# Chunked attention and a Mish feed-forward layer: accumulators copied out one at a time, an earlier load of q and k, and attention steps moved by half a slot

## The chip, the cores and the metric

The kernel runs on one core of one Trainium2 chip. The metric is the device time of one execution in microseconds, the median of several runs. The engines are called by their names in the profile: PE is TensorE, PEld its weight loads, DVE is VectorE, ACT is ScalarE, SP is SyncE, which issues nearly all DMAs here (SPq is its queue of DMA issues), and POOL is GpSimd, which only makes the identity matrix.

## The reference

q, k and v are 8 x 8 heads x 576 positions x 64, in float32. Attention works in chunks of 64 positions that see only themselves; its output, laid out as 4608 tokens of 512, goes through a feed-forward layer of width 2048:

```python
scores = scale * np.matmul(q_c, k_c.transpose(0, 1, 2, 4, 3))
scores = scores - np.max(scores, axis=-1, keepdims=True)
attn = np.exp(scores)
attn = attn / (np.sum(attn, axis=-1, keepdims=True) + 1e-09)
out = np.matmul(attn, v_c)
...
h = x @ w_in
sp = np.where(h > 20.0, h, np.log1p(np.exp(np.minimum(h, 20.0))))
g = h * np.tanh(sp)
return (g @ w_out).astype(np.float32)
```

## The kernel before

**Precision.** The large matmuls take operands in a rounded float32 (fp32r). Each operand is split into a high part (a cast) and a low part (a subtraction), and a product takes three matmuls: low x high, high x low, high x high. So each tile of activations costs one cast and one subtraction of 128x512 before PE can use it. The names end accordingly: `gh` and `gl` are the two parts of the activated hidden tile g, `wo_h` and `wo_l` those of w_out.

**Tiles and blocks.** A pair is 256 tokens; there are 18 pairs. The hidden layer has 16 tiles of 128 (f = 0 to 15). The work goes by blocks of tokens: a first block of pairs 0 and 1 (512 tokens), then blocks 1 to 4 with four pairs (1024 tokens) each.

*The first block* is `prologue` (attention of pairs 0 and 1, first weights) and 16 calls of `slot` (L583 to L622). Each slot does one f: a matmul chain `up` (L419) makes h, ACT applies Mish, `g_split` (L434) makes gh and gl, and `down` queues 12 matmuls (4 token tiles t = 0 to 3 times three parts) that add g @ w_out into the accumulators. Beside that the slot takes in the weights: they come as 64-bit words, ACT scales, DVE puts bits together (`w_bits`, L116), ACT casts the high part, DVE subtracts for the low part (`w_lo`, L140). The attention of pairs 2 to 5, which block 1 needs, is spread over the slots as well. Its steps stand in two plans, `on_pe` and `beside_pe` (L555 to L577), whose keys count half slots: scores, max and subtraction (L254, L266), exponential (L275), sum and reciprocal (L280), normalisation `a_norm` (L287), transposes `a_transpose` (L296), their copy out `a_copy` (ps, L307), the product with v `a_values` (av, L228) and its copy out `a_raw` (raw, L317).

*Blocks 1 to 4* replace the plain product x @ w_in by a scheme with seven products of half size (`PRODUCTS`, L626) on sums of parts of x (`x_step`: splits x_B, x_T at L373 and L374, sums raw at L379) and of parts of the weights. `s_build(u)` (L183) makes the weight sums for unit u: four DVE operations (L196), an ACT cast (L198), a DVE subtraction (L199) and a store, all in one buffer `bld`. `load_op` (L640) loads one operand of the products, from the plain parts (w_A) or the sums (w_S). Per block there are 8 calls of `unit` (L671), each for two f and both halves of the block's tokens. A unit's seven products go to three PSUM tiles in turn, x, y and v, from a pool of two; ACT copies x out (L682, L704, L716), DVE adds y and v to what was copied (`add`, L666), and ACT applies Mish (L432). Between the products a unit works off the queue `fill` by `filled(n)` (L465): n of the matmuls that earlier `down` calls queued. They belong to the first half of the block's tokens; the second half's activations stay in the buffer `zb` until `phase_two` (L746), which takes them f by f. In blocks 1 to 3 the units also carry the attention of the next block's pairs (one pair for two units), and `phase_two` its x_steps.

**Accumulators.** `acc[0]` to `acc[3]` are the four token tiles of the half in work. They lie in two PSUM tiles of two banks each: o0 holds t = 0 and 1, o2 holds t = 2 and 3, as these lines of `down_mm` show:

```python
if f == 0 and n == 0 and t % 2 == 0:
    o = ps_o.tile([P, 2, DM], F32, name=f"o_{key}_{t}", tag=f"o{t}")
    acc[t], acc[t + 1] = o[:, 0], o[:, 1]
```

`store` (L469) copies all four out to buffers `ob`, even t on ACT (L475), odd t on DVE (L473), and sends each with two DMAs on SP's queue (L479). The buffers are from the pool `c` with three buffers. It is called in unit 0 of each block, after the fifth product and ahead of `a_norm` (for the second half of the block before), in `phase_two` at f = 1 (for the first half), and at the end.

**Order.** The kernel runs under a manual schedule: each engine, and SP's queue, works in the order in which the code issues, and the framework adds the semaphore waits. q, k, v, p and ps of most pairs share the pool `at` with three buffers.

## Time and profile before

| | |
|---|---|
| median of 3 runs | 900.29 us (899.21 to 901.59) |
| the profiled execution, its own time | 900.59 us |
| its span, first to last instruction | 898.8 us |
| mean granted PE clock | 0.969 |
| ACT busy | 387.9 us (43%) |
| DMA, mean over the span | 153 GB/s, 137.25 MB |

The stages, by stretches of the span, with PE's busy time, the time that it stands still, DVE's and ACT's busy time (us) and PE's granted clock:

| stretch | what runs | PE | idle | DVE | ACT | clock |
|---|---|---|---|---|---|---|
| 0 to 54 | prologue, slots 0 to 2 | 35.44 | 18.56 | 40.23 | 35.56 | 0.88 |
| 54 to 160 | the other slots | 82.56 | 23.44 | 87.87 | 73.96 | 0.90 |
| 160 to 186 | start and unit 0 of block 1 | 18.13 | 7.87 | 10.45 | 8.42 | 0.83 |
| 186 to 306 | units of block 1 | 118.83 | 1.17 | 60.36 | 52.31 | 0.99 |
| 306 to 318 | start of its second half | 10.43 | 1.57 | 7.16 | 4.58 | 1.00 |
| 351 to 371 | start and unit 0 of block 2 | 16.47 | 3.53 | 9.83 | 8.73 | 1.00 |
| 371 to 489 | units of block 2 | 117.97 | 0.03 | 46.13 | 47.88 | 1.00 |
| 489 to 500 | start of its second half | 9.41 | 1.59 | 6.20 | 4.87 | 1.00 |
| 535 to 555 | start and unit 0 of block 3 | 16.45 | 3.55 | 10.56 | 8.45 | 0.96 |
| 680 to 690 | start of its second half | 8.37 | 1.63 | 6.61 | 3.39 | 1.00 |
| 842 to 852 | the same in block 4 | 8.55 | 1.45 | 3.04 | 2.94 | 1.00 |
| 852 to 899 | the end | 39.89 | 7.11 | 10.85 | 9.28 | 0.96 |

A row of the timeline gives start and length in us, engine, line, operation, output<-inputs, sizes and the number of instructions taken together; in square brackets stands how long the engine had stood idle just before, and what released it. A row of the list of waits gives the waiting engine and line, what it waited for, the total in us, how many times, and the longest. A row of a group gives line, engine, operation, count, busy time and mean of one in ns, then the idle time just before and its releasers.

### The profile page before, as it was taken

To read this page: it belongs to the slowest core of one execution; us is meant where nothing else is said; L and a number is where in the kernel's file an instruction comes from. 1 tells how busy PE (TensorE), PEld (TensorE's weight loads), DVE (VectorE), ACT (ScalarE), POOL (GpSimd) and SP (SyncE) were. 2 spreads that over 40 slices of the span, in tenths; PEclk is the share of its full clock that TensorE was granted. 3 is DMA by queue.
4 is the path that set the end of the run, shared out by engine and by line. 5 is a ranking of instruction groups with operands and counts; after the bars stand their busy time and mean duration, and the time that the engine had idled before them with its cause. 6 is when DMAs were issued, how large, how long until landed. Compare 5 with 4: busy or idle time off the path is not lost.

```text
span 898.8 us, 14182 instructions
## 1 busy us (share of the span) xinstructions
PE 827.2 (92%) x5724; PEld 675.1 (75%) x5724; DVE 438.7 (49%) x678; ACT 387.9 (43%) x584; POOL 0.7 (0%) x6
## 2 busy tenths in 40 slices
PE   4979974689999999899999998999999999999996
PEld 4757763567888788688888786888887888888785
DVE  6878997357435364442443644335336532323322
ACT  4778964335444343443443434344334332222221
POOL 0000000000000000000000000000000000000000
PEclk9889988799999999999999998999999999999999
DMA  7879944599855421656553305555532045444202
GB/s 269 321 266 324 314 171 170 170 303 306 273 159 137 107 66 48 182 140 174 161 140 96 94 19 146 176 153 141 177 107 70 1 115 153 128 120 118 47 1 47
DMA packets 68577, 137.25 MB, mean 153 GB/s; under 512 B 7072, under 2 KB 13216, under 8 KB 67488
## 3 DMA queue, kind: packets, MB, share of 16 engines
q1 hardware_dynamic: 68224, 135.82, 49.8%
q8 instruction: 46, 0.75, 0.3%
q10 hardware_dynamic: 288, 0.52, 0.2%
q14 instruction: 19, 0.16, 0.1%
HBM read 108.00 MB, written 28.31 MB: 152 GB/s over the span
## 4 chain that ended last, share of the span: by engine, by line
PE 77%; DVE 9%; ACT 6%; DMA 5%; issue 3%; SPq 0%; DVEq 0%; ACTq 0%
PE x L654 18%; PE v L654 9%; PE y L654 5%; PE o_(4, 0)_0_6431 L452 2%; PE o_(3, 0)_0_4943 L452 2%; PE o_(1, 1)_2_2947 L452 2%; PE o_(3, 1)_2_6043 L452 2%; PE o_(2, 1)_2_4495 L452 2%; PE o_(4, 1)_2_7188 L452 2%; PE o_(3, 0)_2_4960 L452 2%; PE o_(2, 0)_2_3412 L452 2%; PE o_(4, 1)_0_7181 L452 2%; PE o_(2, 0)_0_3395 L452 2%; PE o_(4, 0)_2_6448 L452 2%; PE av L228 2%
## 5 line engine op out<-in xcount | busy, mean ns | idle before, releaser
L666 DVE TENSOR_TENSOR zb<-v,zb 128x512 f32<-128x512 f32 x64 | 44.2, 690 | 121.2 <-ACT zb L716 64.1
L654 PE MATMUL x<-x_T,w_S 128*128 128x512 f32 x384 | 99.2, 394 | 0.6 <-ACT zb L704 0.6
L654 PEld LDWEIGHTS x<-x_T,w_S 128*128 128x128 f32 x384 | 71.1, 188 | 16.1 <-ACT zb L704 1.1
L666 DVE TENSOR_TENSOR z<-y,z 128x512 f32<-128x512 f32 x32 | 22.1, 692 | 101.3 <-PE y L654 99.3
L432 ACT ACTIVATE zb<-zb 128x512 f32<-128x512 f32 x64 | 40.5, 632 | 70.8 <-DVE zb L666 70.7
L439 DVE CAST gh<-z 128x512 fp32r<-128x512 f32 x72 | 30.6, 425 | 67.0 <-PE o_(4, 0)_2_6448 L452 19.0
L441 DVE TENSOR_TENSOR gl<-z,gh 128x512 fp32r<-128x512 f32 x80 | 55.3, 692 | 13.7 <-ACT gh L437 11.2
L716 ACT COPY zb<-x 128x512 f32<-128x512 f32 x32 | 18.8, 586 | 95.6 <-PE x L654 95.6
L432 ACT ACTIVATE z<-z 128x512 f32<-128x512 f32 x32 | 20.2, 631 | 91.9 <-DVE z L666 91.9
L296 PE MATMUL pt<-ident,p 128*128 128x128 f32 x144 | 23.7, 315 | 32.7 <-DVE p L287 18.9
L654 PE MATMUL x<-x_B,w_A 128*128 128x512 f32 x192 | 52.6, 410 | 0.9 <-ACT x_B L373 0.7
L654 PE MATMUL y<-x_B,w_A 128*128 128x512 f32 x192 | 51.6, 405 | 0.6 <-DVE zb L666 0.6
L419 PE MATMUL h<-x_first,wi 128*128 128x512 f32 (+1 forms) x204 | 50.5, 401 | 0.7 <-ACT x_first L336 0.7
L654 PE MATMUL v<-x_B,w_S 128*128 128x512 f32 x192 | 48.9, 390 | 0.2 <-DVE zb L666 0.2
L654 PE MATMUL x<-x_T,w_A 128*128 128x512 f32 x192 | 48.9, 390 | 0.1
L654 PE MATMUL v<-x_T,w_S 128*128 128x512 f32 x192 | 48.7, 389 | 0.0
L296 PEld LDWEIGHTS pt<-ident,p 128*128 128x128 f32 x144 | 19.4, 162 | 37.7 <-issue 22.9
L419 PEld LDWEIGHTS h<-x_first,wi 128*128 128x128 f32 x204 | 39.0, 206 | 8.4 <-ACT x_first L336 0.9
L654 PEld LDWEIGHTS y<-x_B,w_A 128*128 128x128 f32 x192 | 35.8, 193 | 9.6 <-DVE zb L666 1.8
L654 PEld LDWEIGHTS x<-x_B,w_A 128*128 128x128 f32 x192 | 36.4, 196 | 8.7 <-ACT x_B L373 1.1
L228 PE MATMUL s<-k,q 64*64 64x64 f32 x1088 | 21.7, 232 | 22.7 <-DMA k<-in_k 22.6
L654 PEld LDWEIGHTS v<-x_B,w_S 128*128 128x128 f32 x192 | 36.0, 188 | 8.0 <-DVE zb L666 0.6
(197 smaller groups left out, 1770.3 us busy)
## 6 DMA issues: line engine op xcount, KB each, us to landing
w_S<-sa SPq DMA_DIRECT2D x128, 256.0 KB, 3.2
w_A<-ra SPq DMA_DIRECT2D x96, 256.0 KB, 2.7
wst<-in_w_in SPq DMA_DIRECT2D x16, 512.0 KB, 5.5
wst<-in_w_out SPq DMA_DIRECT2D x16, 512.0 KB, 5.2
q<-in_q SPq DMA_DIRECT2D x16, 512.0 KB, 4.0
k<-in_k SPq DMA_DIRECT2D x16, 512.0 KB, 4.6
v<-in_v SPq DMA_DIRECT2D x16, 512.0 KB, 4.7
sa<-bld SPq DMA_DIRECT2D x8, 1024.0 KB, 5.0
```

The source lines that it names most:

```text
L228: nc.tensor.matmul(o[h * CHUNK : (h + 1) * CHUNK, c, t - ts.start, g], lhsT=l[rows, t, 2 * g + h], rhs=r[rows, t, 2 * g + h], start=True, ...
L296: nc.tensor.transpose(out=d["pt", ts.start][:, t - ts.start, g], in_=d["p"][:, t, g].rearrange("p c k -> p (c k)"), identity=ident,)
L419: nc.tensor.matmul(h[:, cols], lhsT=wi[i][:, w_, kt], rhs=x[:, x_, kt, cols], start=(n == 0), stop=(n == 3 * NK - 1),)
L432: nc.scalar.activation(out=out_, in_=in_, func=AF.Mish)
L439: nc.vector.tensor_copy(out=d["gh"], in_=z)
L441: nc.vector.tensor_tensor(out=d["gl"], in0=z, in1=d["gh"].bitcast(F32), op=ALU.subtract)
L452: nc.tensor.matmul(acc[t], lhsT=g[:, t * P : (t + 1) * P], rhs=w_[:, f], start=(f == 0 and n == 0), stop=(f == NF - 1 and n == 2),)
L654: nc.tensor.matmul(o, lhsT=t[:, w_, kt], rhs=x[x_][:, kt], start=(start and i == 0), stop=(i == 5), skip_group_check=not start,)
L666: nc.vector.tensor_tensor(out=z, in0=o, in1=z, op=ALU.add)
L716: nc.scalar.copy(out=b2, in_=x)
```

## The change

1. **Copies out.** `store` takes one t. In unit 0 of a block the matmuls still in `fill` (24 in block 1, 12 in the others) are spread over the first five products (3, 3, 2, 2 and 2 twelfths), and `stores`, called at four places, copies out each accumulator whose last matmul has been issued. In block 1 that is t = 0 behind `a_exp` and the other three behind `a_norm`; in blocks 2 to 4 t = 0 behind the first copy, t = 1 behind `a_exp`, the other two behind `a_norm`. In `phase_two` at f = 0 the last 12 matmuls of the first half are issued three at a time, each three followed by the copy of their accumulator. At the end the last 24 matmuls are sorted by token tile; six are issued, then that accumulator is copied in two halves, one on ACT and one on DVE, ACT's half with its own DMAs on ACT's queue.
2. **g_split earlier.** In `phase_two` each f's `g_split` stands ahead of the 12 matmuls of the f before it; in every unit the second `g_split` stands ahead of the unit's last `add` and Mish.
3. **q and k of the first pair of block 2** (pair 6) are loaded at the end of slot 14, ahead of both `s_build` calls and of four `load_op`; before, behind `s_build(1)` at the end of slot 15. The half slot's attention steps stand ahead of `s_build` too.
4. **Half a slot.** Transposes, ps, av and raw of pair 2 and all steps of pairs 3 to 5 (the load of their q and k too) come one key, that is half a slot, later, and so does the first part of the steps on x's second half.
5. **Which engine casts gh in the slots.** Before ACT in even slots; now in the slots of `BY_SCALAR`.

```diff
-    def store(key, pairs):
-        for t in range(TOK // P):
...
+    def by_token():
+        fill.sort(key=lambda x: x[3])
+
+    stored = {}
+
+    def stores(key, pairs):
+        done = TOK // P - -(-len(fill) // 3)
+        for t in range(stored.setdefault(key, 0), done):
+            store(key, pairs, t)
+            stored[key] += 1
+
+    def store(key, pairs, t, cuts=1):
+        o = c_p.tile([P, DM], F32, name=f"ob_{key}_{t}", tag="c")
+        half, c = divmod(t, 2)
+        for n in range(cuts):
+            cols = slice(n * DM // cuts, (n + 1) * DM // cuts)
+            on_vector = (t + n) % 2
+            if on_vector:
+                nc.vector.tensor_copy(out=o[:, cols], in_=acc[t][:, cols])
             else:
-                nc.scalar.copy(out=o, in_=acc[t])
...
+                nc.scalar.copy(out=o[:, cols], in_=acc[t][:, cols])
+            queue = nc.scalar if cuts > 1 and not on_vector else nc.sync
...
-    for i, h0 in enumerate((1, 8, 15, 22)):
+    for i, (h0, h1) in enumerate(((1, 7), (9, 14), (16, 21), (23, 28))):
...
-    beside_pe.setdefault(29, []).extend((lambda n: x_step(1, 1, n), n) for n in range(5))
+    beside_pe.setdefault(30, []).extend((lambda n: x_step(1, 1, n), n) for n in range(5))
...
+    BY_SCALAR = (1, 3, 5, 7, 8, 10, 12, 14)
...
-        g_split(it[s], it[s]["z"], f"0_{s}", s % 2 == 0)
+        g_split(it[s], it[s]["z"], f"0_{s}", s in BY_SCALAR)
...
+        run(beside_pe, 2 * s + 1)
         if s == NF - 2:
+            load_qk(first_pair(2))
             s_build(0)
             for i in range(LOOK - 2):
                 load_op()
-        run(beside_pe, 2 * s + 1)
         if s == NF - 1:
             s_build(1)
-            load_qk(first_pair(2))
...
+            parts = [left * n // 12 for n in (3, 3, 2, 2, 2)]
...
         if begins:
             a_scores(j)
             load_v(j)
+        if u == 0:
+            stores(key, pairs)
...
         if begins:
             a_exp(j)
+        if u == 0:
+            stores(key, pairs)
...
-        if u == 0:
-            if m == 1:
-                store("0", (0, 1))
-            else:
-                p = first_pair(m - 1)
-                store(f"{m - 1}b", (p + 1, p + 3))
         if begins:
             a_norm(j)
+        if u == 0:
+            stores(key, pairs)
         product(m, u, 5, x, False)
         a2["z"] = z_tile(f"z_{m}_{2 * u + 1}")
         mish(a2["z"], x)
+        if u == 0:
+            stores(key, pairs)
...
         filled()
+        g_split(a2, a2["z"], f"{m}_{2 * u + 1}")
         add(y, b1)
         mish(b1, b1)
-        g_split(a2, a2["z"], f"{m}_{2 * u + 1}")
...
-            filled(12)
-            if f == 1:
-                store(f"{m}a", (p, p + 2))
             d = {}
+            if f == 0:
+                filled(12)
             g_split(d, z_of(f), f"{m}b_{f}", True)
+            if f == 0:
+                for t in range(TOK // P):
+                    filled(3)
+                    store(f"{m}a", (p, p + 2), t)
+            elif after or f < NF - 1:
+                filled(12)
...
-        filled()
+        by_token()
         p = first_pair(QUADS)
-        store("last", (p + 1, p + 3))
+        for t in range(TOK // P):
+            filled(6)
+            store("last", (p + 1, p + 3), t, 2)
```

The order on DVE at the end of the slots, slots 14 and 15, before. `woc` and `wo_l` (L116, L140) are the last tiles of w_out, p at L287 is pair 5's, raw, x_T and x_B belong to the second half of block 1's x, L196 and L199 are the first weight sums:

```order
L287 TENSOR_TENSOR p_1361<-p_1361,r_0_1416 128x2x8x64
L116 SCALAR_TENSOR_TENSOR woc_1446<-woc_1446,wst 128x512
L116 SCALAR_TENSOR_TENSOR woc_1446<-wst,woc_1446 128x512
L140 TENSOR_TENSOR wo_l<-woc_1409,wo_h 128x512
L374 TENSOR_TENSOR x_T_1_1490<-raw_715,x_T_0_1488 128x4x2x64
L441 TENSOR_TENSOR gl_14_1541<-z_1474,gh_14_1539 128x512
L140 TENSOR_TENSOR wo_l<-woc_1446,wo_h 128x512
L196 TENSOR_TENSOR bld<-bld 128x256 x4
L199 TENSOR_TENSOR bld<-bld 128x4x256
L374 TENSOR_TENSOR x_T_1_1578<-raw_715,x_T_0_1576 128x4x2x64
L374 TENSOR_TENSOR x_B_1_1166<-raw_1266,x_B_0_1164 128x4x2x64
```

and the same stretch in the changed kernel:

```order
L116 SCALAR_TENSOR_TENSOR woc_1442<-woc_1442,wst 128x512
L116 SCALAR_TENSOR_TENSOR woc_1442<-wst,woc_1442 128x512
L140 TENSOR_TENSOR wo_l<-woc_1408,wo_h 128x512
L287 TENSOR_TENSOR p_1390<-p_1390,r_0_1448 128x2x8x64
L374 TENSOR_TENSOR x_T_1_1479<-raw_741,x_T_0_1477 128x4x2x64
L441 TENSOR_TENSOR gl_14_1506<-z_1464,gh_14_1504 128x512
L140 TENSOR_TENSOR wo_l<-woc_1442,wo_h 128x512
L374 TENSOR_TENSOR x_T_1_1562<-raw_741,x_T_0_1560 128x4x2x64
L196 TENSOR_TENSOR bld<-bld 128x256 x4
L199 TENSOR_TENSOR bld<-bld 128x4x256
L439 CAST gh_15_1584<-z_1556 128x512
L441 TENSOR_TENSOR gl_15_1586<-z_1556,gh_15_1584 128x512
```

p of pair 5 (L287) now stands behind the two bit operations and one subtraction more. The second x_T, which stood behind the sums, stands ahead of them, and behind the sums come gh and gl of slot 15, whose cast was on ACT before.

The order on PE at the start of block 1's second half, with the semaphores that are waited for. o_(1, 0)_0 holds accumulators 0 and 1, o_(1, 0)_2 accumulators 2 and 3; the rows are the last matmuls of the first half (f = 15), three for each accumulator. Before:

```order
L452 MATMUL o_(1, 0)_0_1808<-wo_h_98,gl_1_15_2877 128x512 [waits DVE_49]
L452 MATMUL o_(1, 0)_0_1808<-wo_l_99,gh_1_15_2875 128x512
L452 MATMUL o_(1, 0)_0_1808<-wo_h_98,gh_1_15_2875 128x512
L452 MATMUL o_(1, 0)_0_1808<-wo_h_98,gl_1_15_2877 128x512
L452 MATMUL o_(1, 0)_0_1808<-wo_l_99,gh_1_15_2875 128x512
L452 MATMUL o_(1, 0)_0_1808<-wo_h_98,gh_1_15_2875 128x512
L452 MATMUL o_(1, 0)_2_1825<-wo_h_98,gl_1_15_2877 128x512
```

and changed:

```order
L452 MATMUL o_(1, 0)_0_1808<-wo_h_98,gl_1_15_2875 128x512 [waits DVE_49]
L452 MATMUL o_(1, 0)_0_1808<-wo_l_99,gh_1_15_2873 128x512
L452 MATMUL o_(1, 0)_0_1808<-wo_h_98,gh_1_15_2873 128x512
L452 MATMUL o_(1, 0)_0_1808<-wo_h_98,gl_1_15_2875 128x512 [waits Activation_49]
L452 MATMUL o_(1, 0)_0_1808<-wo_l_99,gh_1_15_2873 128x512
L452 MATMUL o_(1, 0)_0_1808<-wo_h_98,gh_1_15_2873 128x512
L452 MATMUL o_(1, 0)_2_1825<-wo_h_98,gl_1_15_2875 128x512
```

Between the third and the fourth row, from accumulator 0 to accumulator 1, PE now waits for a semaphore of ACT. The same stands between accumulators 2 and 3.

The order on DVE at the end of unit 1 of block 1. The first `zb` belongs to the sum that frees v's bank, gh_1_3 and gl_1_3 to the unit's second tile. Before:

```order
L196 TENSOR_TENSOR bld_1484<-bld_1484 128x256 x4
L199 TENSOR_TENSOR bld_1484<-bld_1484 128x4x256
L666 TENSOR_TENSOR zb_1_0_1614<-v_1_1_1890,zb_1_0_1614 128x512
L439 CAST gh_1_3_1954<-z_1_3_1931 128x512
L441 TENSOR_TENSOR gl_1_3_1956<-z_1_3_1931,gh_1_3_1954 128x512
L666 TENSOR_TENSOR z_1_4_1958<-y_1_2_2007,z_1_4_1958 128x512
```

and changed:

```order
L196 TENSOR_TENSOR bld_1474<-bld_1474 128x256 x4
L199 TENSOR_TENSOR bld_1474<-bld_1474 128x4x256
L439 CAST gh_1_3_1952<-z_1_3_1931 128x512
L441 TENSOR_TENSOR gl_1_3_1954<-z_1_3_1931,gh_1_3_1952 128x512
L682 TENSOR_TENSOR zb_1_0_1614<-v_1_1_1890,zb_1_0_1614 128x512
L682 TENSOR_TENSOR z_1_4_1958<-y_1_2_2007,z_1_4_1958 128x512
```

The cast and the subtraction for gh and gl now stand ahead of the add to zb.

More of the change, by code (lines that the diff above doesn't have):

```diff
@@ L467, in filled @@
             down_mm(*fill.pop(0))
-    def store(key, pairs):
-        for t in range(TOK // P):
-            o = c_p.tile([P, DM], F32, name=f"ob_{key}_{t}", tag="c")
-            if t % 2:
-                nc.vector.tensor_copy(out=o, in_=acc[t])
-            else:
-                nc.scalar.copy(out=o, in_=acc[t])
-            half, c = divmod(t, 2)
+    def by_token():
[14 more added lines that the diff above has]
+                nc.vector.tensor_copy(out=o[:, cols], in_=acc[t][:, cols])
+            else:
+                nc.scalar.copy(out=o[:, cols], in_=acc[t][:, cols])
+            queue = nc.scalar if cuts > 1 and not on_vector else nc.sync
             for i in range(2):
                 r = (pairs[half] * 2 + i) * P + c * CHUNK
-                nc.sync.dma_start(
-                    out=out[r : r + CHUNK, :], in_=o[i * CHUNK : (i + 1) * CHUNK]
+                queue.dma_start(
+                    out=out[r : r + CHUNK, cols], in_=o[i * CHUNK : (i + 1) * CHUNK, cols]
                 )
@@ L555 @@
     on_pe, beside_pe = {}, {}
-    for i, h0 in enumerate((1, 8, 15, 22)):
+    for i, (h0, h1) in enumerate(((1, 7), (9, 14), (16, 21), (23, 28))):
         j = first_pair(1) + i
-        for n, step in ((0, a_scores), (5, a_transpose), (6, a_values)):
+        for n, step in ((0, a_scores), (h1 - h0, a_transpose), (h1 - h0 + 1, a_values)):
             on_pe.setdefault(h0 + n, []).append((step, j))
@@ L565 @@
             (4, (a_norm,)),
-            (5, (a_copy,)),
-            (6, (a_raw,)),
+            (h1 - h0, (a_copy,)),
+            (h1 - h0 + 1, (a_raw,)),
         ):
@@ L677, in unit @@
         a1, a2 = {"z": z_tile(f"z_{m}_{2 * u}")}, {}
+        left = len(fill)
+        if u == 0:
+            parts = [left * n // 12 for n in (3, 3, 2, 2, 2)]
+            if m == 1:
+                key, pairs = "0", (0, 1)
+            else:
+                p = first_pair(m - 1)
+                key, pairs = f"{m - 1}b", (p + 1, p + 3)
         x = ps_h.tile([P, TOK], F32, name=f"x_{m}_{u}", tag="h")
         product(m, u, 0, x, True)
-        filled(3)
+        filled(parts[0] if u == 0 else 3)
         nc.scalar.copy(out=a1["z"], in_=x)
@@ L685, in unit @@
             load_v(j)
+        if u == 0:
+            stores(key, pairs)
         y = ps_h.tile([P, TOK], F32, name=f"y_{m}_{u}", tag="h")
         product(m, u, 1, y, True)
-        filled(5)
+        filled(parts[1] if u == 0 else 5)
         add(y, a1["z"])
@@ L702, in unit @@
         product(m, u, 2, x, False)
-        filled(4)
+        filled(parts[2] if u == 0 else 4)
         nc.scalar.copy(out=b1, in_=x)
@@ L706, in unit @@
             a_exp(j)
+        if u == 0:
+            stores(key, pairs)
         y = ps_h.tile([P, TOK], F32, name=f"v_{m}_{u}", tag="h")
         product(m, u, 3, y, True)
-        filled(4)
+        filled(parts[3] if u == 0 else 4)
         g_split(a1, a1["z"], f"{m}_{2 * u}")
@@ L729, in unit @@
         mish(a2["z"], x)
+        if u == 0:
+            stores(key, pairs)
         if m == 1 and (u, 1) in BUILDS:
```

## The prediction

> **What bounds the kernel now.** I read the busy times first, then the list of who waited for whom, then the instructions in order of time where PE (TensorE) stands still. In the first fence come the page's busy line, then wait rows: engine and line, what it waited for, total us, times, longest.
>
> ```profile
> PE 827.2 (92%) x5724; PEld 675.1 (75%) x5724; DVE 438.7 (49%) x678; ACT 387.9 (43%) x584; POOL 0.7 (0%) x6
> ...
> PE s L228 <- DMA k<-in_k: 22.6, 2, 17.9
> PE pt L296 <- DVE p L287: 18.9, 5, 5.9
> PE o_(4, 1)_2_7188 L452 <- DVE ob_4a L473: 1.4, 1, 1.4
> PE o_(1, 1)_2_2947 L452 <- DVE ob_1a L473: 1.0, 1, 1.0
> PE o_(1, 1)_0_2940 L452 <- DVE ob_1a L473: 0.5, 1, 0.5
> DVE gl L441 <- ACT gh L437: 11.2, 5, 4.3
> ```
>
> PE is busy 827.2 of 898.8 us, and its number of matmuls does not change, so only the 71.6 us of standing still can be won (and what a slowed clock costs behind them). The largest wait is one of 17.9 us for k, then the transposes that wait for the normalised p (DVE, VectorE). The copies of the accumulators cost PE little directly, about 1.5 us at each of four places, but DVE waits inside them. In the first block PE waits for DVE, and DVE in turn stands 11.2 us for casts on ACT (ScalarE). Times are summed against the profiled execution, 900.6 us (span 898.8 and 1.8 around it); the median of the runs, 900.29, is 0.3 lower.
>
> **Part 1: k, and what is late behind it.** The instructions around the wait (start, us, engine, line; in brackets idle time before and its releaser):
>
> ```profile
> 131.94 1.22 DVE L287 TENSOR_TENSOR p<-p,r 128x1024 f32<-128x1024 f32 x1
> 133.31 1.94 PE L296 MATMUL pt<-ident,p 128*128 128x128 f32 x8 [5.93 <-DVE p L287]
> 134.90 3.98 PE L419 MATMUL h<-x_first,wi 128*128 128x512 f32 x12
> 138.80 1.16 PE L228 MATMUL av<-ps,v 64*64 64x64 f32 x64
> 140.03 1.01 ACT L317 COPY raw<-av 128x1024 f32<-128x1024 f32 x1 [2.18 <-PE av L228]
> 142.37 0.63 ACT L373 CAST x_T<-raw 128x512 fp32r<-128x512 f32 x1
> 149.82 2.50 DVE L374 TENSOR_TENSOR x_T<-raw,x_T 128x512 fp32r<-128x512 f32 x4
> 152.24 1.55 DVE L196 TENSOR_TENSOR bld<-bld 128x256 f32<-128x256 f32 x4
> 153.87 1.04 ACT L198 CAST bld<-bld 128x1024 fp32r<-128x1024 f32 x1 [2.52 <-issue]
> 154.94 1.22 DVE L199 TENSOR_TENSOR bld<-bld 128x1024 fp32r<-128x1024 f32 x1 [1.15 <-ACT bld L198]
> 157.03 0.95 SPq L211 DMA_DIRECT2D k<-in_k  x1
> 164.31 1.98 PE L228 MATMUL s<-k,q 64*64 64x64 f32 x64 [17.86 <-DMA k<-in_k]
> 168.69 0.69 DVE L666 TENSOR_TENSOR z<-y,z 128x512 f32<-128x512 f32 x1 [12.52 <-PE y L654]
> ```
>
> k's load went out at 157.03, behind the store of the second weight sums, and PE could start at 164.31: 7.3 us. Now q and k stand on SP's queue before the second load of bld, the first store of sums and three loads of w_S; they wait only for the buffers of pair 5, the last of them free after av of pair 5. What they are put ahead of waits for DVE's sums, which come later anyway, so their issue costs nothing. PE needs k some 9 us after that av (next paragraph): the wait goes. What is late next is DVE. It ended the second sums at 156.2 and then had nothing to do until 168.7, when it added y to z. With all else equal that add would come 12.5 us sooner: **+12.5** (a gain is +).
>
> The half slot works against it here. The DVE order puts p's normalisation behind two bit operations and a subtraction more (3 x 0.69, as the other rows of that size): it ends at 131.94 + 1.22 + 2.1 = 135.2. The last split of the first half (x_T) and the sums now stand behind raw, and raw behind pt, the 12 accumulator matmuls and av. From the rows: pt to the next matmul 1.6, 12 matmuls behind such a stall 3.9, so av at 140.8; raw ends 2.2 later, the cast 0.6 and the split 0.7 after that: 144.3. Then in DVE's order sums 1.55, ACT's cast 1.04, L199 1.22, gh and gl of slot 15 1.1, three x_B at the 0.63 of an x_T 1.9, four raw sums 2.8 (0.69 each, as the add at 168.69), x_T 2.5, sums, cast and L199 again 3.9: 160.4 in place of 156.2: **-4.2** (bounds: 0, if DVE has caught up earlier, and -7, if ACT holds the casts up too).
>
> Earlier in the first block the half slot should help. DVE's three longest waits there, and the size of a cast on it:
>
> ```profile
> 32.49 0.69 DVE L441 TENSOR_TENSOR gl<-z,gh 128x512 fp32r<-128x512 f32 x1 [2.54 <-ACT gh L437]
> 46.95 0.69 DVE L441 TENSOR_TENSOR gl<-z,gh 128x512 fp32r<-128x512 f32 x1 [2.58 <-ACT gh L437]
> 63.41 0.69 DVE L441 TENSOR_TENSOR gl<-z,gh 128x512 fp32r<-128x512 f32 x1 [4.27 <-ACT gh L437]
> L439 DVE CAST gh<-z 128x512 fp32r<-128x512 f32 x72 | 30.6, 425 | 67.0 <-PE o_(4, 0)_2_6448 L452 19.0 <-PE o_(3, 0)_2_4960 L452 17.1 <-PE o_(2, 0)_2_3412 L452 17.1
> ```
>
> They are slots 0, 2 and 4, where DVE now makes gh itself for 0.43 each: 9.4 - 1.3 = 8.1. Following the new orders with these durations up to 70 us I find four smaller waits for ACT in their place (0.3, 0.7, 0.5, and 1.7 for the gh of slot 5 behind raw's copy): 4.9 is left, and as DVE stays the fullest engine up to the end of the slots, I take it as lasting: **+4.9** (bounds 0, if ACT's queue eats all, and 8.1). The transposes of pair 2 and the one at 133.31 still wait for DVE. The add thus comes at 155.5: part 1 is +13.2.
>
> **Part 2: unit 0 of each block, where copies stood ahead of p's normalisation.**
>
> ```profile
> 173.01 1.06 ACT L275 ACTIVATE p<-p 128x1024 f32<-128x1024 f32 x1
> 174.10 1.22 DVE L280 TENSOR_REDUCE r<-p 128x16 f32<-128x1024 f32 x1 [0.86 <-ACT p L275]
> 188.25 1.56 PE L654 MATMUL y<-x_B,w_A 128*128 128x512 f32 x6
> 369.06 0.69 DVE L473 COPY ob_1b<-o_(1, 1)_2_2947 128x512 f32<-128x512 f32 x1 [2.35 <-DMA out<-ob_1b]
> 371.03 1.06 PE L296 MATMUL pt<-ident,p 128*128 128x128 f32 x8 [3.56 <-DVE p L287]
> 374.00 1.52 PE L654 MATMUL y<-x_B,w_A 128*128 128x512 f32 x6
> 554.30 1.94 PE L296 MATMUL pt<-ident,p 128*128 128x128 f32 x8 [3.55 <-DVE p L287]
> 559.88 1.76 PE L654 MATMUL y<-x_B,w_A 128*128 128x512 f32 x6
> ```
>
> DVE's copy of the fourth accumulator waits 2.35 us for the DMA that empties the first one's buffer (there are three), and p waits behind it. Now p comes first. In blocks 2 and 3 PE's 3.56 and 3.55 go; the 12 matmuls that moved out of unit 0 leave about 0.3 of new waiting for ACT's copies: 3.2 each. In block 3 the stall also slowed the clock: from pt to the next unit's y 5.58 against 2.97 in block 2, 2.6 more. **+9.0** (6 to 10).
>
> TensorE: Matmul & The Clock Gate (the Trainium skill, section "What's actually happening") says that about 3.4 us of idleness halve the clock, in a window that runs freely, so a stall hardly longer may or may not fill one; the two equal stalls, with 1.06 and 1.94 us of transposes behind them, agree. By it alone block 2's stall would have an even chance to cost 2.6 as well, and the term would be 10.3.
>
> In block 1 I follow unit 0 from its add. Before, y of unit 1 came 188.25 - 168.69 = 19.6 later. Now, in us after the add's start: add, max and subtraction (1.22 each, the size of the sums) 3.1, exp 4.3. The copy of accumulator 0 sits behind that exp on ACT, and the next accumulator matmul waits for it: 4.9; four matmuls, product 4 and the copy of b2 7.8; add and normalisation 9.7, two copies 11.0, sums, cast and L199 14.9, gh, gl and the add that frees y's bank 16.7: **+2.9** (1 to 4).
>
> **Part 3: gh and gl ahead of the last add.** In every unit y of the next unit needs the bank that this add frees. In units 1 and 2 of block 1 DVE arrives there late already:
>
> ```profile
> 204.90 0.68 DVE L666 TENSOR_TENSOR zb<-v,zb 128x512 f32<-128x512 f32 x1
> 205.77 1.66 PE L654 MATMUL y<-x_B,w_A 128*128 128x512 f32 x6
> 765.71 0.39 PE L452 MATMUL o_(4, 0)_2_6448<-wo_h,gh 128*128 128x512 f32 x1
> 767.97 1.52 PE L654 MATMUL y<-x_B,w_A 128*128 128x512 f32 x6
> ```
>
> y starts 0.2 after the add's end; 0.43 + 0.69 ahead of it cost PE 1.1 in both: **-2.2** (0 to -2.5). In block 4, which has no attention between, gh waits for the last accumulator matmul (766.1), and gh, gl and add then end at 767.9; y started at 767.97: 0.1 in six units, **-0.6** (0 to -1.5). With attention between there is 0.8 more room, so 0.
>
> **Part 4: the copies one by one.** The PE order shows a wait for ACT between accumulator 0 and 1, and between 2 and 3: the next matmul of the pair waits until its neighbour is copied.
>
> ```profile
> 309.80 0.58 ACT L475 COPY ob_1a<-o_(1, 0)_0_1808 128x512 f32<-128x512 f32 x1
> 886.48 0.62 ACT L437 CAST gh_4b<-zb 128x512 fp32r<-128x512 f32 x1 [2.10 <-PE o_(4, 1)_2_7188 L452]
> 891.50 0.39 PE L452 MATMUL o_(4, 1)_2_7188<-wo_h,gh_4b 128*128 128x512 f32 x1
> 894.23 0.69 DVE L473 COPY ob_last<-o_(4, 1)_2_7188 128x512 f32<-128x512 f32 x1 [2.35 <-DMA out<-ob_last]
> ```
>
> One such wait: matmul 0.39, copy 0.58, about 0.1 around it, less the 0.23 from one matmul's start to the next (six take 1.52, of which the last 0.39): 0.85. Two at the start of each block's second half: 1.7 x 4 = 6.8, and 0.3 in three blocks for a gl that now stands behind two splits, in place of 6.1 (the wait rows give 1.5 in block 1 and 1.4 in block 4; blocks 2 and 3 are taken as block 1): **-1.6** (+6.1 to -3).
>
> At the end PE stops at 891.9, the span ends 6.9 later, 3.9 of it behind the last copy. Now the halves of a bank are copied one after the other (the second waits for the first): about 0.4 each, estimated from half of 0.58 and 0.69 and a start, so the tail is 0.9 + 3.9 = 4.8, 2.1 less. Against it two waits between neighbours (0.85 + 0.3 each), and 0.9 because gl of the last f, ready 1.4 after the matmuls that free its gh (0.62 + 0.69 and a gap), is wanted 0.5 after them, behind three matmuls instead of twelve: **-1.1** (+2 to -2).
>
> **Sum.** 13.2 + 9.0 + 2.9 - 2.2 - 0.6 - 1.6 - 1.1 = 19.6; 900.6 - 19.6 = **881.0 us**.
>
> **Rivals.** *A: the copies run beside the next matmuls.* Then part 4's neighbour waits (6.8 + 2.3) are not there: 872. For it: the accumulators are separate banks, and the wait rows show no PE wait inside a pair; against it: the order's wait. Chance 0.07. PSUM — Partial Sum Buffer (the Trainium skill, "Summary: rules for kernel authors") asks only for a different bank to read while a matmul runs, which would give A; no row of before has a copy beside matmuls of its own pair.
> *B: the half slot gains nothing.* DVE's waits move to other casts, so +4.9 is 0, and the chain at the slots' end is at its bound of -7: 889. For it: all of DVE's 11.2 us for gh come from ACT's queue, which keeps the copies ps and raw, only elsewhere. Against it: three waits of a cast each go for certain, since DVE makes it itself. Chance 0.18.
> *C: slower.* gh and gl delay y in all 32 units, not in the nine counted: if gh waits for accumulator matmuls that end 1.9 us later than I take them (0.8 of room and the 1.1 of gh and gl), the other 23 units lose 1.1 each, 25 us, and 906 results; it makes the kernel slower from 0.85 us a unit. Against it: those matmuls stand right behind the unit's last product. Chance 0.03.
>
> **How the numbers follow.** My case 0.70, A 0.07, B 0.18, C 0.03; 0.02 for several terms failing together near no change. 0.3% (2.7 us) is what a measurement of this kernel can tell. Faster 0.95, same 0.02, slower 0.03. The range reaches from A to just beyond B, which also holds the unknown costs of my case: 871 to 890.
>
> **What would show it.** Right: no wait for k over 1 us; pt in unit 0 of blocks 2 and 3 without a wait; DVE's second sums near 155; PE waits of 0.7 for ob inside a pair at each second half. Wrong: a long wait for p at pair 5 that grows past 8 us; PE running through the pairs (A); y waiting for zb in most units (C).

## The result and the profile after

The changed kernel takes 887.62 us (median of 4 runs, 883.94 to 887.81) against 900.46 for the kernel before in the same session: ratio 0.985, 95% interval 0.982 to 0.988, faster by 1.5%. The forecast was 881.0, range 871 to 890. The profiled execution took 887.46 us (span 885.4, granted clock 0.978; before 900.59, 898.8 and 0.969).

The busy line of the page, and then rows of the list of waits (engine and line, what it waited for, total us, times, longest):

```profile
PE 832.3 (94%) x5724; PEld 674.4 (76%) x5724; DVE 436.0 (49%) x680; ACT 385.0 (43%) x586; POOL 0.7 (0%) x6
```

```profile
DVE x_T L374 <- ACT x_T L373: 6.9, 2, 6.5
DVE gl L441 <- ACT gh L437: 6.5, 4, 2.8
PE pt L296 <- DVE p L287: 7.6, 4, 3.4
PE y L670 <- DVE zb L682: 5.5, 3, 2.9
PE x L670 <- ACT x_B L373: 5.4, 1, 5.4
PE s L228 <- DMA k<-in_k: 4.9, 1, 4.9
PE o_(1, 0)_0_1808 L452 <- ACT ob_1a L489: 0.7, 1, 0.7
PE o_(1, 0)_2_1825 L452 <- ACT ob_1a L489: 0.7, 1, 0.7
```

The wait of 17.9 us for k is gone (the 4.9 left are the first load of the kernel), and the waits for p fell from 18.9 to 7.6. Two others have grown: 5.4 for x_B (0.7 before) and 5.5 for y's bank (0.6 before). The two of 0.7 for ACT's copies are new, and they stand in blocks 2 to 4 as well. PE's busy time rose by 5.1 us with the same 5724 matmuls, since more of them ran at a low clock: 49 of the 128x512 matmuls took 0.6 us or more in this execution, and 32 before. (The clock averaged over the span rose all the same, from 0.969 to 0.978.)

To see where the time went, I take the start of DVE's first add of a unit (z<-y,z) in both traces. It marks PE's progress:

| place | before | changed | shift | shift in a second profiled execution of the changed kernel |
|---|---|---|---|---|
| block 1, unit 0 | 168.69 | 160.63 | -8.1 | -10.4 |
| block 1, unit 1 | 190.09 | 179.93 | -10.2 | -12.6 |
| block 1, unit 3 | 226.02 | 219.29 | -6.7 | -9.9 |
| block 2, unit 1 | 375.63 | 365.64 | -10.0 | -13.2 |
| block 3, unit 1 | 561.74 | 545.68 | -16.1 | -19.3 |
| block 4, unit 1 | 739.68 | 723.53 | -16.2 | -19.3 |
| block 4, unit 7 | 829.44 | 814.33 | -15.1 | -18.3 |
| end of the span | 898.8 | 885.4 | -13.4 | -15.8 |

So the first block and k brought 8 to 10 us, units 1 and 2 of block 1 gave 2.6 to 3.4 back, unit 0 of blocks 2 and 3 brought 9.3, and block 4 and the end gave 2.8 to 3.5 back. The two executions differ by 2.4 us where block 1 begins, and by at most 0.8 more behind it.

The end of the slots in the changed kernel (start, us, engine, line; in brackets the idle time before and its releaser):

```profile
141.49 1.16 PE L228 MATMUL av<-ps,v 64*64 64x64 f32 x64
142.71 1.01 ACT L317 COPY raw<-av 128x1024 f32<-128x1024 f32 x1 [3.95 <-PE av L228]
143.62 0.62 ACT L373 CAST x_T<-raw 128x512 fp32r<-128x512 f32 x1
144.28 0.69 DVE L374 TENSOR_TENSOR x_T<-raw,x_T 128x512 fp32r<-128x512 f32 x1 [6.47 <-ACT x_T L373]
144.89 1.54 DVE L196 TENSOR_TENSOR bld<-bld 128x256 f32<-128x256 f32 x4
146.46 1.04 ACT L198 CAST bld<-bld 128x1024 fp32r<-128x1024 f32 x1 [2.22 <-DVE bld L196]
147.41 1.66 ACT L373 CAST x_B<-raw 128x512 fp32r<-128x512 f32 x3
148.08 2.08 PE L670 MATMUL x<-x_B,w_A 128*128 128x512 f32 x4 [5.43 <-ACT x_B L373]
160.63 0.68 DVE L682 TENSOR_TENSOR z<-y,z 128x512 f32<-128x512 f32 x1
```

DVE stands 6.47 us for the cast of x_T, with the weight sums queued behind it. ACT cannot cast those sums until they are made, and the casts of x_B, for which PE waits 5.43 us, stand behind that cast.

### The profile page after: what moved, and what is told of

Read it like the earlier page. It is cut to its first block, busy times and chain, and to the rows that moved or that the text cites. A ratio compares the mean times of both kernels' runs of the same rounds, so it can differ in the third digit from the quotient of the medians.

```text
span 885.4 us, 14202 instructions
## 1 busy us (share of the span) xinstructions
PE 832.3 (94%) x5724; PEld 674.4 (76%) x5724; DVE 436.0 (49%) x680; ACT 385.0 (43%) x586; POOL 0.7 (0%) x6
## 4 chain that ended last, share of the span: by engine, by line
PE 77%; DVE 8%; ACT 4%; issue 2%; DMA 2%; ACTq 0%; SPq 0%; DVEq 0%
PE x L670 18%; PE v L670 9%; PE y L670 5%; PE o_(2, 0)_2_3412 L452 2%; PE o_(3, 0)_2_4960 L452 2%; PE o_(4, 0)_2_6448 L452 2%; PE o_(4, 0)_0_6431 L452 2%; PE o_(3, 0)_0_4943 L452 2%; PE o_(2, 0)_0_3395 L452 2%; PE o_(3, 1)_0_6031 L452 2%; PE o_(1, 1)_0_2935 L452 2%; PE o_(2, 1)_0_4483 L452 2%; PE o_(4, 1)_0_7181 L452 2%; PE o_(1, 1)_2_2942 L452 2%; PE o_(3, 1)_2_6038 L452 2%; PE o_(2, 1)_2_4490 L452 2%
## 5 line engine op out<-in xcount | busy, mean ns | idle before, releaser
L670 PEld LDWEIGHTS x<-x_T,w_A 128*128 128x128 f32 x192 | 35.6, 188 | 9.8 <-ACT zb L745 2.6
L670 PEld LDWEIGHTS v<-x_T,w_S 128*128 128x128 f32 x192 | 36.0, 188 | 7.5
L296 PE MATMUL pt<-ident,p 128*128 128x128 f32 x144 | 21.9, 298 | 14.8 <-DVE p L287 7.6
```

The lines of the kernel that those rows point to most:

```text
L296: nc.tensor.transpose(out=d["pt", ts.start][:, t - ts.start, g], in_=d["p"][:, t, g].rearrange("p c k -> p (c k)"), identity=ident,)
L670: nc.tensor.matmul(o, lhsT=t[:, w_, kt], rhs=x[x_][:, kt], start=(start and i == 0), stop=(i == 5), skip_group_check=not start,)
```

## The experiments

Each was timed in three rounds beside the kernel before; medians are of four runs. The changed kernel itself ran twice, eight executions in all, from 883.94 to 887.81 us.

### The early load alone

```diff
         if s == NF - 2:
+            load_qk(first_pair(2))
             s_build(0)
...
             s_build(1)
-            load_qk(first_pair(2))
```

> The kernel before with one edit: q and k of pair 6 are loaded at the end of slot 14, ahead of the first weight sums. Theory (the load alone is worth what the prediction gave it): the 17.9 us wait for k goes, what is late next is DVE's second sums, and the first add of block 1 comes 12.5 us sooner than in the kernel before, so about 888 us (886 to 890), as fast as the whole changed kernel; the half slot, the copies and the splits together then bring nothing. Rival (the load was only half of it, because the place is held by the buffers of pair 5 or by the loads behind it on SP): PE still waits over 5 us for k, and the time is 893 us or more.

890.35 us (889.41 to 894.37), ratio 0.988 (0.984 to 0.992), just above the theory's 886 to 890. No wait for k is left in block 1:

```profile
141.14 1.16 PE L228 MATMUL av<-ps,v 64*64 64x64 f32 x64
148.71 1.16 PE L228 MATMUL s<-k,q 64*64 64x64 f32 x64
157.28 1.23 DVE L199 TENSOR_TENSOR bld<-bld 128x1024 fp32r<-128x1024 f32 x1 [1.15 <-ACT bld L198]
158.42 0.68 DVE L666 TENSOR_TENSOR z<-y,z 128x512 f32<-128x512 f32 x1
```

The add comes 10.3 us sooner than before, and 12.6 measured from av of pair 5, which in this execution ran 2.3 later (141.14 against 138.80). The theory's mechanism holds: the wait goes, DVE's second sums are what is late next, and 12.5 was the right price at that place. (The profiled execution is the slowest of the four, 894.37 us: behind this add it loses 4.0 us of the lead again, with a granted clock of 0.5 behind the waits for p in unit 0 of blocks 1 and 2.) The load is also most of what the whole change brings in time (10.1 of 12.8 us).

### The half slot, the order of the sums, and the casts

Without the half slot (plans, casts' engines and order of the sums as before, the load early):

```diff
-    for i, (h0, h1) in enumerate(((1, 7), (9, 14), (16, 21), (23, 28))):
+    for i, (h0, h1) in enumerate(((1, 6), (8, 13), (15, 20), (22, 27))):
...
-    BY_SCALAR = (1, 3, 5, 7, 8, 10, 12, 14)
+    BY_SCALAR = tuple(range(0, 16, 2))
...
```

> The changed kernel without the half slot: attention steps, the steps on x, the casts' engines and the order of the sums at slot 14 as before, the load of q and k stays early. Theory (the half slot costs): the first add of block 1 came 8.1 us sooner in the changed kernel, and it should come 12.5 sooner with the load alone, so this kernel is 4.4 us faster than the changed one, about 883 us. Rival (the prediction: the half slot brings 4.9 us and costs 4.2): no slower or faster than 1 us, 887 to 888 us.

885.61 us (885.04 to 887.12): within the scatter of the changed kernel, so the theory's 883 was missed. The half slot with all that came with it neither gains nor costs what eight executions can tell.

Only the order of the sums put back, so that the half slot stays:

```diff
-        run(beside_pe, 2 * s + 1)
         if s == NF - 2:
             load_qk(first_pair(2))
             s_build(0)
             for i in range(LOOK - 2):
                 load_op()
+        run(beside_pe, 2 * s + 1)
```

> The changed kernel with one edit: at the end of slot 14 the first weight sums stand ahead of raw and the split of x_T again, as before the change. Theory (the sums' new place behind x_T is what costs): DVE waits 6.5 us for the cast of x_T with the sums queued behind it, and ACT's cast of the sums holds up the casts of x_B for which PE waits 5.4 us; with the sums ahead, x_B's cast ends some 3.3 us sooner and DVE's second sums 3.8 us sooner, so about 884 us. Rival (the slots themselves run late by then, and PE is held by p's normalisation): under 1 us, 886.5 to 888 us.

882.84 us (880.13 to 885.03), 4.5 below the median of the changed kernel's eight executions (887.4). The place that waited 5.43 us:

```profile
135.84 1.05 ACT L198 CAST bld<-bld 128x1024 fp32r<-128x1024 f32 x1
140.10 1.01 ACT L317 COPY raw<-av 128x1024 f32<-128x1024 f32 x1 [3.21 <-PE av L228]
141.53 1.66 ACT L373 CAST x_B<-raw 128x512 fp32r<-128x512 f32 x3
142.20 1.20 PE L670 MATMUL x<-x_B,w_A 128*128 128x512 f32 x4 [2.17 <-ACT x_B L373]
154.18 0.68 DVE L682 TENSOR_TENSOR z<-y,z 128x512 f32<-128x512 f32 x1
```

The sums are cast before raw exists, the wait falls to 2.17 as expected, and the first add comes 14.5 us sooner than in the kernel before. With the sums in the same place, the half slot's kernel has that add 3.3 us before the one without it (14.5 against 11.2) and 2.8 us in the medians. So the half slot, with the new engines of its casts, does gain, and the new place of the sums ate it.

Which part of it gains? The same kernel, with ACT casting gh in even slots as before:

> The changed kernel with the first sums ahead of raw and x_T, and with gh cast by ACT in even slots as before the change; the half slot stays. Theory (the lead in the slots comes from the casts that DVE makes itself): gl of slot 4 falls back from 58.4 to some 63 us, the lead at slot 14 goes, and the kernel is 3 us slower than with the first sums alone, about 886 us, as without the half slot. Rival (the later attention steps make the lead, since ACT's copies no longer stand ahead of the casts): gl of slot 4 stays before 60 us, and the time is 883 us.

883.46 us (881.82 to 884.65), not to be told from 882.84. The split of slot 4 starts at 60.7 us, between the theory's 63 and the 58.4 with the new casts, and the first add comes 2.3 us later. In the profile both parts seem to have a share: the split of slot 14 starts at 136.1 us here, at 132.8 with the new casts, and at 139.3 without the half slot. But the clock fell behind different stalls in these executions (from the transposes of pair 4 to their av 5.34 us here and 3.76 with the new casts, at pair 5 5.35 and 6.40), so the shares are rough, and in time it stays open.

### The changed kernel again: the clock

> The changed kernel itself once more, on the chip and in the hours of the next three. Theory (part of what its profiled execution lacks is the clock: the transposes of pair 4 at 107.16 us took 1.94 in place of 1.06, and the scores of pair 5 came 5.4 us later than in the kernel before, while two kernels with the same instructions up to there have them 1.1 and 1.6 later): its executions scatter between 884 and 888 us with the granted clock, and a profiled execution without that slow stretch has the first add of block 1 some 10 us sooner than the kernel before and not 8.1. Rival (a steady property of the kernel): all executions within 1 us of 887.6.

886.59 us (884.97 to 887.68), so executions do scatter, over 2.7 us here and over 3.9 in all eight. The same place in its profile and in the first profile of the changed kernel:

```profile
106.02 1.06 PE L296 MATMUL pt<-ident,p 128*128 128x128 f32 x8 [2.73 <-DVE p L287]
106.84 2.99 PE L419 MATMUL h<-x_first,wi 128*128 128x512 f32 x12
109.76 1.16 PE L228 MATMUL av<-ps,v 64*64 64x64 f32 x64
```

```profile
107.16 1.94 PE L296 MATMUL pt<-ident,p 128*128 128x128 f32 x8 [2.73 <-DVE p L287]
108.75 5.07 PE L419 MATMUL h<-x_first,wi 128*128 128x512 f32 x12
113.75 1.16 PE L228 MATMUL av<-ps,v 64*64 64x64 f32 x64
```

The same stall of 2.73 us is followed by full speed once, and by half speed the other time: 3.74 us to av against 6.59. What decides between the two is in the granted clock. The windows below are of the second profile, then of the first; a row gives start:end and length, busy us and instructions of PE, PEld, DVE, ACT and POOL, then the granted clock, the DMA share and GB/s:

```profile
104.11:107.52 3.41, 1.50 (x11) 1.45 (x12) 3.38 (x6) 2.30 (x5) 0.00 (x0) 1.00 0.85 253
107.52:110.94 3.42, 3.42 (x76) 2.67 (x74) 2.50 (x5) 2.81 (x5) 0.00 (x0) 1.00 0.69 230
```

```profile
102.98:106.39 3.41, 1.45 (x7) 0.87 (x5) 3.38 (x6) 2.76 (x5) 0.00 (x0) 1.00 0.88 307
106.39:109.80 3.41, 2.64 (x11) 2.48 (x12) 2.52 (x4) 1.47 (x3) 0.00 (x0) 0.50 0.66 208
```

In each of the fourteen traces the granted clock changes only at whole multiples of 3.41 us from its other changes, and this grid lies differently against the kernel in every execution. Cut along their grids, the traces hold 3410 such windows at full clock. The next window ran at 0.5 behind each of the 85 in which PE, by its recorded busy time, stood idle for 1.97 us or more, behind none of the 3293 with less than 1.68, and behind 8 of the 32 between. So a stall of 2.73 us slows PE when the grid leaves about 2 us of it in one window, and not when the grid cuts it more evenly. In the eleven traces that have this stall (2.73 or 2.74 us) the clock fell behind it six times. The two shown lie at the border, with 1.96 us idle and 1.91.

The shifts in the table differ by 2.4 us at block 1's first add by three such places: the first profile is 1.1 us behind the second when this stall ends (its clock was low for 6.8 us near 62 us, the second's for 3.4) and 4.0 behind at av. Then it catches up 1.6: PE waits 0.6 less at pair 5, and in the second profile the clock fell behind that wait (6.31 us from the transposes to av, against 5.34).

### The split ahead of the add

```diff
-        g_split(a2, a2["z"], f"{m}_{2 * u + 1}")
         add(y, b1)
         mish(b1, b1)
+        g_split(a2, a2["z"], f"{m}_{2 * u + 1}")
```

> The changed kernel with the last add and Mish of every unit ahead of the second split again, as before the change. Theory (the split ahead of the add delays y's bank): units 1 and 2 of block 1 get back the 3.4 us that the shift between the two traces shows there, and block 4 its 1.0 us, so about 883 us. Rival (the split is needed as early as the add, since the accumulator matmuls of the next unit wait for gl): what y gains is lost at gl, 886.5 to 888 us.

882.47 us (882.24 to 883.79). In block 4 the shift now stays at -20.1 us from unit 1 to unit 7, so the 1.0 came back. From the first add of unit 0 to that of unit 3 of block 1 the kernel takes 57.0 us, the changed one 58.7 and 57.9 in its two profiles: 0.9 to 1.7, not 3.4. The other 2.2 us of its lead lie ahead of block 1, where its instructions are those of the changed kernel: that is the clock again (the second profile of the changed kernel has 10.4 there, this one 10.3). What is left in units 1 and 2 is told by its rows there:

```profile
178.75 1.55 DVE L196 TENSOR_TENSOR bld<-bld 128x256 f32<-128x256 f32 x4 [1.98 <-DMA bld<-cs]
182.74 1.04 ACT L198 CAST bld<-bld 128x1024 fp32r<-128x1024 f32 x1 [3.72 <-DMA sa<-bld]
183.69 0.58 ACT L731 COPY zb<-x 128x512 f32<-128x512 f32 x1
184.33 1.66 PE L670 MATMUL x<-x_T,w_S 128*128 128x512 f32 x6 [1.62 <-ACT zb L731]
```

DVE waits for the load of the next weights, ACT for the store of the last sums, and PE for a copy that is queued behind ACT's wait. What came sooner has to wait for transfers there.

### The copies: own tiles, old end, old place of p

Each accumulator as a PSUM tile of its own:

```diff
...
-        if f == 0 and n == 0 and t % 2 == 0:
-            o = ps_o.tile([P, 2, DM], F32, name=f"o_{key}_{t}", tag=f"o{t}")
-            acc[t], acc[t + 1] = o[:, 0], o[:, 1]
+        if f == 0 and n == 0:
+            acc[t] = ps["o"].tile([P, DM], F32, name=f"o_{key}_{t}", tag=f"o{t}")
...
```

> The changed kernel with one edit: each accumulator is a PSUM tile of its own (one bank), and the prologue's tiles that shared the names come from a pool that ends with the prologue. Theory (PE's 0.7 us waits for ACT's copies come from the two accumulators' being one tile, not from the chip): the eight waits of 0.7 at the starts of the second halves, 1.4 in unit 0 of block 1 and 2.6 at the end go, 9.6 us in all, and nothing else is late there: 878 to 880 us. Rival (a copy out of one bank holds up matmuls into the next, or the next split is late instead): the waits stay or gl takes their place, 885 us or more.

879.88 us (879.08 to 880.71). The start of block 1's second half, first in the changed kernel, then with own tiles:

```profile
302.15 0.59 ACT L489 COPY ob_1a<-o_(1, 0)_0_1808 128x512 f32<-128x512 f32 x1
302.79 0.50 PE L452 MATMUL o_(1, 0)_0_1808<-wo_h,gl 128*128 128x512 f32 x1 [0.68 <-ACT ob_1a L489]
```

```profile
299.99 0.59 ACT L488 COPY ob_1a<-o_(1, 0)_0_1814 128x512 f32<-128x512 f32 x1
300.02 0.39 PE L451 MATMUL o_(1, 0)_1_1828<-wo_l,gh 128*128 128x512 f32 x1
303.61 0.69 DVE L486 COPY ob_1a<-o_(1, 0)_3_1893 128x512 f32<-128x512 f32 x1 [2.25 <-ACT gh_1b L437]
304.36 0.50 PE L451 MATMUL o_(1, 1)_3_2955<-wo_h,gl_1b 128*128 128x512 f32 x1 [0.32 <-DVE ob_1a L486]
306.16 0.50 PE L451 MATMUL o_(1, 1)_0_2943<-wo_h,gl_1b 128*128 128x512 f32 x1 [0.83 <-DVE gl_1b L441]
```

PE now runs on while ACT copies the neighbour: the waits were the program's, made by two accumulators in one tile, not the chip's. PSUM — Partial Sum Buffer (the Trainium skill, "Summary: rules for kernel authors") asks for a different bank when PSUM is read beside a running matmul; the copy at 299.99 beside the matmul at 300.02 agrees. But at the starts 0.3 to 0.5 for the fourth copy and 0.8 for gl take the place of 1.4, and only some 0.4 of each is won: from unit 7 of a block to unit 0 of the next the shift shrinks by 2.3 or 2.4 us where it shrank by 2.7. The larger gain is at the end: from block 4's unit 7 on the changed kernel loses 1.7 (2.5 in its second profile) to the kernel before, and this one gains 1.6. From block 1's first add to the end that makes 4.4 us in the profiles, less than half of the theory's 9.6; that the median fell into its 878 to 880 us is luck in part, by the scatter of the changed kernel.

The end as before the change:

> The changed kernel with the end as before the change: the last matmuls not sorted by token, four whole copies after them, all DMAs on SP's queue. Theory (the new end costs more than it saves): from the first of the last 24 matmuls to the end of the span the changed kernel takes 14.3 us and the kernel before 12.5, so this kernel is 1.8 us faster than the changed one. Rival (the halves save time at the tail, and the loss lies at the start of block 4's second half): as fast as the changed kernel or up to 2 us slower.

882.96 us (882.74 to 883.29). From unit 7 of block 4 to the end it loses nothing to the kernel before, so the new end costs 1.7 to 2.5 with paired tiles; the rest of the 4.4 us in the medians I take as the scatter of the changed kernel. Why it costs stands in the changed kernel's rows:

```profile
874.59 0.50 PE L452 MATMUL o_(4, 1)_0_7181<-wo_h,gl_4b 128*128 128x512 f32 x1 [0.92 <-DVE ob_last L487]
...
877.15 1.15 ACTq L493 DMA_DIRECT2D out<-ob_last  x2
878.42 0.37 ACT L489 COPY ob_last<-o_(4, 1)_2_7188 128x256 f32<-128x256 f32 x1 [1.30 <-PE o_(4, 1)_2_7188 L452]
878.83 0.42 DVE L487 COPY ob_last<-o_(4, 1)_2_7188 128x256 f32<-128x256 f32 x1 [2.11 <-ACT ob_last L489]
879.31 0.50 PE L452 MATMUL o_(4, 1)_2_7188<-wo_h,gl_4b 128*128 128x512 f32 x1 [1.69 <-DVE ob_last L487]
```

ACT spends 1.15 us issuing the two DMAs of one half, with its next copy queued behind them, and PE waits 1.69 for that copy and the other half (0.92 for accumulator 0, where no issue stood ahead of the copy). Without the shared tile PE doesn't wait for these copies, and the same end gains 1.6 us on the kernel before.

In unit 0, the copies due at the fifth product ahead of p's normalisation again:

```diff
-        if begins:
-            a_norm(j)
         if u == 0:
             stores(key, pairs)
+        if begins:
+            a_norm(j)
```

> The changed kernel with one edit: in unit 0 of each block the copies that are due at the fifth product stand ahead of p's normalisation again. Theory (the place of the normalisation brought the gain of unit 0, as the prediction put it): the transposes of blocks 2 and 3 wait for p some 3.5 us again, and the kernel is 6 to 9 us slower than the changed one, 893 us or more. Rival (the gain came from the copies' being spread: accumulators 0 and 1 are copied earlier, so the buffer of the fourth is free and nothing waits for a DMA; one DVE copy of 0.7 ahead of p is hidden or costs 0.7 in three blocks): 887 to 889 us.

888.91 us (888.61 to 888.97): the time that the rival gave, 1.3 and 2.3 above the two medians of the changed kernel. Block 2 in this kernel:

```profile
358.84 0.69 DVE L487 COPY ob_1b<-o_(1, 1)_2_2942 128x512 f32<-128x512 f32 x1 [1.41 <-ACT ob_1b L489]
359.44 1.22 DVE L287 TENSOR_TENSOR p<-p,r 128x1024 f32<-128x1024 f32 x1
360.81 1.06 PE L296 MATMUL pt<-ident,p 128*128 128x128 f32 x8 [1.34 <-DVE p L287]
```

and in the changed one:

```profile
359.12 1.21 DVE L287 TENSOR_TENSOR p<-p,r 128x1024 f32<-128x1024 f32 x1
360.61 0.69 DVE L487 COPY ob_1b<-o_(1, 1)_2_2942 128x512 f32<-128x512 f32 x1 [0.28 <-ACT ob_1b L489]
361.08 1.03 PE L296 MATMUL pt<-ident,p 128*128 128x128 f32 x8
```

In the rows the order is worth 1.5 us in blocks 2 and 3 each, and 0.7 to 1.5 in block 1 up to its unit 3, which is more than the rival gave it and less than the theory. With the order put back, the rest of the 3.2 stays: two accumulators are copied earlier, and no copy in unit 0 waits for a DMA (2.3 to 2.4 before). What the order alone would bring without the earlier copies was not run.

### Together

The first two edits that helped, sums first and add first:

> The changed kernel with both edits that helped alone: the first weight sums ahead of raw and x_T, and the last add of every unit ahead of the second split. Theory (they act at different places and add up: 882.8 for the sums, and 2.7 us for the add, of which 1.7 in units 1 and 2 of block 1 and 1.0 in block 4): 880 us. Rival (in units 1 and 2 of block 1 DVE waits for the loads of the next weights and the stores of the sums, so what comes earlier waits longer there): 882 to 883 us.

879.31 us (878.42 to 881.34): as the theory had it. With own tiles as well:

> The changed kernel with the three edits that helped: first sums ahead of raw and x_T, the add ahead of the second split, an own PSUM tile for each accumulator. Theory (they act at different places): the two edits together had 879.3 us; the own tiles save some 4.1 us at the end and 0.46 at each of four starts of a second half in the profile, 5.9 in all, so 873.4 us. Rival (they share a place, or the next late thing eats it): 876 us or more.

873.31 us (872.7 to 874.07), as expected; ratio 0.969 (0.967 to 0.970) to the kernel before. And with the store of the sums in two parts:

```diff
         nc.scalar.copy(out=o[:, :, 0].bitcast(F32R), in_=s)
+        nc.sync.dma_start(out=sum_ops[u][:, :, 0], in_=o[:, :, 0])
         nc.vector.tensor_tensor(out=o[:, :, 1].bitcast(F32R), in0=s, in1=o[:, :, 0], op=ALU.subtract)
-        nc.sync.dma_start(out=sum_ops[u], in_=o)
+        nc.sync.dma_start(out=sum_ops[u][:, :, 1], in_=o[:, :, 1])
```

> The kernel with the three edits, and the store of each weight sum split in two: the high parts go out right behind ACT's cast, the low parts behind DVE's subtraction, with the same bytes in all. Theory (in units 1 and 2 of block 1 ACT's cast of the next sums waits 1.6 and 2.6 us for the store of the last, with the copy for PE queued behind it): the high parts are free 1.2 us earlier at least, and the kernel is 1 to 3 us faster than the one with the three edits. Rival (the load of the next weights for the sums, also late there, or the transfers' own rate sets the pace): within 0.7 us of it, or slower for its shorter rows.

874.01 us (873.05 to 876.02), the same. ACT's waits for the store, 6.1 us before, are gone from the list of waits, and from unit 0 to unit 3 of block 1 the time is 56.3 us as against 56.4: PE's wait for y in unit 1 grew from 1.88 to 3.13, and its chain from 1.65 to 2.92 at a lower clock. From the first add of unit 0 to that of unit 1 it loses 2.2 us to the kernel without the split store, and from there to unit 3 it wins 2.3. Whether the split store is worth those 2.3 where the clock holds, or the next load sets the pace, stays open.

## Why the prediction was right, and where it was not

The sign, the range and the largest term were right; the sum was 19.6 us where 13.4 came in the profile, and 15.8 in the second. By its steps:

1. **k, +12.5: right.** The early load alone moved the add by 12.6 from av of pair 5.
2. **The casts and the half slot in the slots, +4.9: right where the clock let it.** In the second profile of the changed kernel the split of slot 14 starts at 133.2 us against 137.9, 4.7 sooner; in the first at 136.5, after the slow stretch at 107 us, which I had not counted. The size is right but the cause only in part: I gave all of it to the casts that DVE makes itself, and with ACT casting as before the split of slot 14 still starts at 136.1, so the later attention steps have a share.
3. **The half slot at the slots' end, -4.2: the step that failed, too small.** I counted three DVE operations that p is moved behind. Its sum and reciprocal (L280 to L282, 1.22 + 0.17 + 0.25 = 1.6 us) moved by half a slot too, from ahead of the split of slot 13 to behind it, between that split and p. And I took av to follow the stall in 5.5 us, where it took 6.3 in the second profile, at a granted clock of 0.5. So part 1 brought 10.4 (8.1 with the slow stretch) and not 13.2, and with +12.5 and the lead of 4.7 the half slot cost some 6.8 at the slots' end. I had the waits of x_T, the sums and L199 in a row in the working, and still didn't see that putting them back in the old order was worth 4 us: the half slot's gain was spent there.
4. **Unit 0: right in size.** Block 1 gained 2.1 (2.9 predicted). Blocks 2 and 3, with the starts of second halves between, gained 9.3; 9.0 less half of the 1.6 for the four starts is 8.2. The 2.8 by which block 3 gained more than block 2 are the slowed clock that I had put at 2.6. The prediction gave all of the rest to p's place ahead of the copies; putting p back behind them cost 1.5 of 3.2 in a block, so the earlier copies hold up the other half.
5. **gh and gl ahead of the add: right in size.** -2.8 predicted; putting it back gave 0.9 to 1.7 and 1.0. Rival C, the same in all units, did not come: other units keep their shift to 0.1.
6. **Units 1 and 2 of block 1: not seen.** Their loss of 2.6 to 3.4 is in part the waiting of sums for their transfers.
7. **Copies one by one, -1.6: the rows are right, the sum is too pessimistic.** The waits inside a pair are there, at 0.7 each and not 0.85, and the 0.3 for gl did not come. So the starts cost about 0: 1.4 at each, where the list of waits before has 1.4 to 1.6 (6.1 in all; the 1.5 and 1.4 named in the working add up to 5.9), and block 3's second half and block 4's unit 0 together shift by 0.1. Rival A fell for this kernel, and own tiles show that its mechanism is right without the shared tile.
8. **The end, -1.1: right in sign, 1.7 to 2.5 in size.** I had not counted the DMAs that ACT now issues between its copies. (The 2.5 is of the second profile, where the granted clock was 0.5 for 3.4 us there.)

Rival B's 889 is nearer to the measured time than my 881, but half of its reason falls: DVE's lead of 4.7 us at slot 14 was there. The other half came: the chain at the slots' end came near its bound of -7, and the lead came to nothing in it.

## What to carry to other kernels

When a step is moved by half a stage, list everything on its way, not only what it is moved past: its own reductions, the steps that follow its result, and what is queued behind those. An early step whose input comes late belongs behind a step whose input is ready; here putting the ready sums first was worth over 4 us. Two results that are drained one by one need a tile each, or the drain of one stops the writer of the other.

## What was not expected of the hardware

A stall of 2.73 us was followed by half speed in one execution and by full speed in another (6.59 and 3.74 us for the same instructions). The clock was set window by window, on a grid of 3.41 us, and 1.97 us of idle PE in one window were enough for 0.5 in the next, 85 times out of 85. TensorE: Matmul & The Clock Gate (the Trainium skill, "What's actually happening") tells of a free-running window of about 3.4 us and puts the low clock behind an idle one; the grid agrees, but here the window did not have to be idle throughout. The windows also explain the two equal stalls of the prediction: the grid cut block 2's 3.56 us into 1.69 and 1.87, and the transposes kept 1.06 us, while block 3's 3.55 led to 1.94. The even chance that the prediction took from the Trainium skill was too low. In the six stalls of 3.55 to 3.57 us in unit 0 of blocks 1 to 3, in the kernel before and in the early load's, the clock fell behind five; by the windows a stall of that length escapes about one time in ten, an estimate from the 3.41 and the 1.97.

Such stalls make executions of one kernel differ by some us (2.4 at block 1's first add between the two profiles of the changed kernel), so a part worth 2 us is better read from the shift between two places of a profile than from the time.
